# A linear-attention plus routed-MLP kernel: expert 0's first layer in batches of three, its weights fetched ahead of the last values, and a new written-out order

## The chip, the cores and the metric

The program runs on one core of one Trainium2 chip. That core has a matrix engine (TensorE, PE in the profile; PEld is its weight loads), a vector engine (VectorE, DVE), a scalar engine (ScalarE, ACT), a general engine that here issues nearly all transfers (GpSimd, POOL) and a small engine that issues the first few (SyncE, SP). The metric is the device time of one execution in microseconds; lower is better. The time before is 220.91 us, the median of 3 runs (220.52 to 221.06).

## What is computed

Two stages, one behind the other. The first is an attention without a score matrix: `q` is softened over the 64 features of a head, `k` over the 576 positions, and the product of `k` and `v` is one 64x64 matrix for each batch and head.

```
q_s = exp(q - max(q, -1)); q_s = q_s / (sum(q_s, -1) + 1e-09)
k_s = exp(k - max(k, 2));  k_s = k_s / (sum(k_s, 2) + 1e-09)
kv  = einsum('bhsd,bhse->bhde', k_s, v)
x   = einsum('bhsd,bhde->bhse', q_s, kv)          # 8 batches, 8 heads, 576 positions, 64
```

The second takes the 4608 rows of `x` (512 wide), gives each to one of 8 experts by a hash of its token's number, and runs that expert's two layers.

```
expert_idx = token_ids * 2654435761 % 8
for e in range(8):
    mask = expert_idx == e
    out[mask] = maximum(x[mask] @ w1[e], 0) @ w2[e]     # w1 512x1024, w2 1024x512
```

## The kernel before

Queries are never processed in their own order. The hash is ranked first (`_Index`), and the rows of `q` are gathered by expert: each expert has room for 640 rows, 72 from each of the 8 batches (576, `MAINC`) and 64 more (columns 576 to 640) for rows that exceed a batch's 72. These overflow rows come from four gathers of their own (expert "O"), are multiplied with their batch's key-value matrix in `overflow` and spread over the experts by one-hot matrices `Q` (`shared`, `spread`, `join`).

For a batch `b`, `K` and `V` load the keys and values, `EK` is the exponential on ACT, `KV` the 20 matmuls of keys with values (`keys`), and `SC` the division by the sums that leaves `kvr` (`scaled`, four DVE instructions). The sums come from a 129th column of ones beside each 128 value columns; `MK` (`mark`) writes that column on ACT. For an expert `e`, `G` are the gathers of 128 queries, `EQ` the exponentials, `SM` and `ML` the sums and the division on DVE, `TP` and `TC` the transposes on PE and their copies into `qT`, `PP` and `PC` the products with `kvr` and their copies into `XT`. `A` and `R` are the first layer and its relu (`first`, `relu`), `B` and `C` the second layer and its copy (`second`, `result`), `S` the scatter of 128 rows to the output.

Transfers of weights, `W<expert><layer>_<half>`, cast float32 to half precision in flight. The exponentials of the keys are stored in the tiles that later hold expert 1's weights. `ANY` is a branch into a slow path for the case that more than 64 rows overflow; each engine reads a flag, made in `CNT`, and jumps over that path. What is issued behind the branch waits until the engines that it depends on have passed the branch too.

All engines are scheduled by hand: the table `ORDER` lists some 700 steps, and each engine gets its instructions in the order in which the steps stand there. A name with `*n` puts n extra matmuls of 512 columns ahead of the step; their results are overwritten (`bank`). `SWAP` lists the copies that go to the other one of ACT and DVE. POOL therefore issues transfers strictly in the table's order, and each of its eight transfer semaphores is used again only when the transfer eight places earlier has landed.

PSUM has two buffers for each of three tags: "Q" and "T" (one bank each) and "S" (two banks: `keys`, and the first layer's larger pieces).

Expert 0's first layer is cut in columns 0 to 432 (four pieces `A0_0_0` to `A0_0_3`, eight matmuls each of 432 columns), 432 to 576 and 576 to 640. The first cut needs batches 0 to 5 and both halves of the weights.

Of the kernel before, what the change touches and what calls it, by code (L numbers as in the profile page):

```python
# [21 lines left out]
E_MOE = 8  # L22
# [285 lines left out]
class _Attention:  # L308

    def __init__(self, nc, tc, q, k, v, cpool, qpool, apool, ps):  # L310
# [4 lines left out]
        self.two = cpool.tile([128, VW - 128], F16, name="two")  # L315
        nc.vector.memset(self.two[:], 1.0)
# [118 lines left out]

    def product(self, qT, r, lo, hi, es, q0=0):
# [121 lines left out]
def _any_routing(nc, tc, q, k, v, token_ids, w1, w2, room, ident, w, ps, pool, out):  # L558
# [40 lines left out]
    with tc.For_i(0, NBP, 1) as n:  # L599
# [9 lines left out]
        nc.vector.memset(v16[:, :, 128:VW], 1.0)  # L609
# [17 lines left out]
        with tc.For_i(0, C9, 1) as c:  # L627
# [60 lines left out]
TC1_0 SD1 PC0_00 SD2 TCO_3 PC0_43 PC0_62 R0_0_3 TC2_0 C0_3 TC3_2 PC2_01 C0_0 PC2_02 C0_1 R1_320_1 C0_2 PC2_30  # L688
PC2_61 C2_0 PC4_31 C2_4 C4_2 PC6_31 C6_4 R7_0_0 C7_4a C7_4b
# [56 lines left out]
def kernel(  # L746
# [13 lines left out]
    with ExitStack() as fctx:  # L760
# [19 lines left out]
        with tc.manual_schedule(engines={eng.Pool, eng.PE, eng.DVE, eng.Activation}):  # L780
# [268 lines left out]
```

## Time and profile before

| what | value |
|---|---|
| median of 3 runs | 220.91 us |
| time of the profiled execution | 221.03 us |
| its span, first to last instruction | 219.3 us |
| PE busy | 187.9 us (86%) |
| DVE busy | 132.1 us (60%) |
| ACT busy | 114.8 us (52%) |
| POOL busy | 114.7 us (52%) |
| mean granted TensorE clock | 0.988 |
| bytes read from memory, written to it | 63.03 MB, 10.49 MB |

The span splits in two. Up to about 62 us the keys, values, queries and the first weights arrive, and all engines have gaps. From there to the last matmul PE has none. In the rows below "busy" of a group of matmuls includes the emptying of the pipeline, so that the time of one is read from the distance between starts, or from the chain of waits, which gives the undisturbed length of a piece. A transfer's row gives its size and the time from issue to landing; its issue stands in the rows of POOL.

### The profile page before, as it was taken

The page shows a single profiled execution, that of the slowest core. Times are in us where ns is not written, and L with a number is a line of the kernel's source. Part 1 is how long each engine was busy: PE and PEld are TensorE (multiplying, and loading weights), DVE is VectorE, ACT ScalarE, POOL GpSimd, SP SyncE. Part 2 cuts the span into 40 slices and gives each one's busy share as a digit, 9 for nine tenths or more (in the row PEclk, how much of TensorE's full clock was granted, in tenths as well). Part 3 has the DMA queues.
Part 4 walks back from the last instruction along what each step waited for, and adds up shares of the span by engine and source line. Part 5 has one row for each costly group of instructions (what it writes and reads, how often), then busy time and mean ns, then how long its engine had stood idle before and what let it go on. Part 6 is the DMA issues. An engine that isn't in the chain of part 4 may idle for free.

```text
span 219.3 us, 3984 instructions
## 1 busy us (share of the span) xinstructions
PE 187.9 (86%) x1534; PEld 122.0 (56%) x1534; DVE 132.1 (60%) x258; ACT 114.8 (52%) x184; POOL 114.7 (52%) x152
## 2 busy tenths in 40 slices
PE   3601098679899999999999999999999999999991
PEld 2501186347756865646676555667665566665540
DVE  6889689989969884659984505696324322021330
ACT  8125995799766674646465572436342432622201
POOL 7577876076367475558245407816055140833553
PEclk9999999699999999999999999999999999999998
DMA  6999999999999999999999924999769968595243
GB/s 207 308 324 314 335 396 384 227 326 306 231 336 258 269 247 319 293 216 200 249 209 212 206 80 83 211 219 269 176 145 226 237 144 187 144 167 212 96 153 119
DMA packets 12904, 50.64 MB, mean 231 GB/s; under 512 B 2522, under 2 KB 2522, under 8 KB 11344
## 3 DMA queue, kind: packets, MB, share of 16 engines
q0 software_dynamic: 12304, 46.63, 82.2%
q1 hardware_dynamic: 576, 3.71, 4.4%
q8 instruction: 13, 0.21, 0.4%
q14 instruction: 11, 0.09, 0.1%
HBM read 63.03 MB, written 10.49 MB: 335 GB/s over the span
## 4 chain that ended last, share of the span: by engine, by line
PE 64%; DVE 10%; issue 5%; POOL 4%; ACT 2%; POOLq 1%; DVEq 0%
PE ph L523 30%; PE po L545 25%; POOL out_dram L550 4%; PE t L432 3%; DVE kvr L388 2%; DVE qs L422 2%; PE px L455 2%; DVE rq L416 2%; PE t L443 2%; PE t L373 1%; ACT w1r L355 1%; PE t L472 1%; DVE XT L942 1%; DVE Q L280 1%; DVE XTov L478 1%
## 5 line engine op out<-in xcount | busy, mean ns | idle before, releaser
L545 PE MATMUL po<-w2r,hT 128*128 128x512 f16 (+2 forms) x328 | 74.6, 374 | 0.0
L523 PE MATMUL ph<-XT,w1r 128*128 128x320 f16 (+2 forms) x512 | 74.3, 298 | 0.0
L550 POOL DMA_INDIRECT out_dram<-ob,sidx x40 | 40.8, 1020 | 54.8 <-DVE ob L973 37.7
L536 ACT ACTIVATE hT<-ph 128x640 f16<-128x640 f32 (+3 forms) x60 | 42.4, 708 | 49.0 <-PE ph L523 48.9
L523 PEld LDWEIGHTS <-w1r 128*128 128x128 f16 x544 | 49.1, 98 | 20.7
L396 POOL DMA_INDIRECT raw<-in_q_dram,gidx x36 | 39.5, 1097 | 21.4 <-issue 6.8
L545 PEld LDWEIGHTS <-hT 128*128 128x128 f16 x328 | 31.1, 98 | 30.8
L973 DVE TENSOR_SCALAR ob<-po 128x512 f32<-128x512 f32 x31 | 21.1, 687 | 44.5 <-PE po L545 41.7
L416 DVE TENSOR_REDUCE rq<-qs 128x16 f32<-128x1024 f16 (+1 forms) x18 | 23.9, 1329 | 4.8 <-ACT qs L406 4.6
L406 ACT ACTIVATE qs<-raw 128x512 f16<-128x512 f32 x36 | 22.1, 630 | 5.6 <-DMA raw<-in_q_dram,gidx 4.8
L422 DVE TENSOR_TENSOR qs<-qs,rq 128x1024 f16<-128x1024 f16 (+1 forms) x18 | 23.9, 1326 | 0.1
L912 DVE COPY qT<-t 128x512 f16<-128x512 f16 (+1 forms) x18 | 9.3, 533 | 12.4 <-PE t L432 12.4
L432 PE MATMUL t<-ident,qs 128*128 128x128 f16 x160 | 14.2, 226 | 2.9 <-DVE qs L422 2.3
L432 PEld LDWEIGHTS <-qs 128*128 128x128 f16 x160 | 11.2, 101 | 5.2 <-ACT qs L406 2.5
L508 POOL DMA_DIRECT2D w2r<-in_moe_w_dram x14 | 8.2, 590 | 9.1 <-PE po L545 8.5
L948 ACT CAST XT<-px 128x864 f16<-128x864 f32 (+1 forms) x8 | 6.4, 819 | 11.6 <-PE px L455 11.5
L971 ACT ACTIVATE ob<-po 128x512 f32<-128x512 f32 (+2 forms) x10 | 5.5, 557 | 13.1 <-PE po L545 11.4
L355 ACT ACTIVATE w1r<-kraw 128x2048 f16<-128x2048 f32 x4 | 7.6, 1906 | 8.8 <-DMA kraw<-in_k_dram 8.8
L508 POOL DMA_DIRECT2D w1r<-in_moe_w_dram x15 | 8.8, 587 | 3.7 <-PE ph L523 2.0
L373 PE MATMUL t<-v,w1r 128*128 128x129 f16 x64 | 6.0, 244 | 5.4 <-ACTq L852 5.4
L942 DVE CAST XT<-t 128x288 f16<-128x288 f32 (+2 forms) x17 | 7.6, 459 | 4.4 <-PE t L443 4.3
L443 PE MATMUL t<-qT,kvr 128*128 128x72 f16 (+1 forms) x96 | 8.5, 206 | 1.0 <-DVE XT L942 0.7
(128 smaller groups left out, 186.2 us busy)
## 6 DMA issues: line engine op xcount, KB each, us to landing
w1r<-in_moe_w_dram POOLq DMA_DIRECT2D x14, 512.0 KB, 8.2
w2r<-in_moe_w_dram POOLq DMA_DIRECT2D x12, 512.0 KB, 9.2
kraw<-in_k_dram POOLq DMA_DIRECT2D x3, 1024.0 KB, 9.1
kraw<-in_k_dram SPq DMA_DIRECT2D x2, 1280.0 KB, 11.7
kraw<-in_k_dram POOLq DMA_DIRECT2D x2, 1280.0 KB, 10.9
w2r<-in_moe_w_dram POOLq DMA_DIRECT2D x2, 1024.0 KB, 9.4
v<-in_v_dram POOLq DMA_DIRECT2D x3, 645.0 KB, 8.2
v<-in_v_dram POOLq DMA_DIRECT2D x3, 516.0 KB, 10.3
```

Of the source, the lines that this page charges most:

```text
L396: nc.gpsimd.indirect_dma_start(out=raw[:, :], out_offset=None, in_=self.q[:, :], in_offset=bass.IndirectOffsetOnAxis(ap=idx[:, i:i + 1], a ...
L406: self.nc.scalar.activation(q16[:, i].rearrange("p h d -> p (h d)"), raws[i][:, :], ACT.Exp)
L416: nc.vector.reduce_sum(rv, qv, axis=AX.X)
L422: nc.vector.tensor_tensor(out=qf, in0=qf, in1=rv.rearrange("p i h -> p (i h)").unsqueeze(2) .to_broadcast([128, (hi - lo) * H_, DH_]), op= ...
L432: nc.tensor.transpose(pv[:, r, 128 * j:128 * j + 128], rq16[1][:, i + j, 2 * r:2 * r + 2, :] .rearrange("p h d -> p (h d)"), self.ident[:])
L443: nc.tensor.matmul(pv[:, :, i * CELL:(i + 1) * CELL], lhsT=self.kvrs[b][:, r, :], rhs=qT[:, r, q0 + es.start:q0 + es.stop, b * CELL:(b + 1 ...
L508: self.nc.gpsimd.dma_start(w[what - 1][:, f], src[e, :, f])
L523: nc.tensor.matmul(p, lhsT=w1r[:, dc, f[i] * 128:(f[i] + 1) * 128], rhs=X[:, dc, :], start=(dc == 0), stop=(dc == DC - 1))
L536: self.nc.scalar.activation(to, fro, ACT.Relu)
L545: nc.tensor.matmul(po[:, 0:d.stop - d.start], lhsT=hT[:, fc, blk * 128:(blk + 1) * 128], rhs=w2r[:, fc, d], start=(fc == 0), stop=(fc == F ...
L550: sc = self.nc.gpsimd.indirect_dma_start(out=self.out[:, :], out_offset=bass.IndirectOffsetOnAxis(ap=self.ix.sidx[:, e, blk:blk + 1], axis=0),
L973: nc.vector.tensor_scalar(out=obs[e, blk][:, d], in0=po[e, blk, x][:, 0:d.stop - d.start], scalar1=1.0 / SX, scalar2=None, op0=ALU.mult)
```

## The change

- **Order.** The table is another one, written anew from start to end. Expert 0's two `w1` transfers stand right behind `V4` and ahead of `V5`, `K6`, `K7`, `V6` and `V7`; before they stood behind all of them. The branch `ANY` stands ahead of `OHA` and `FND` (the search for overflow rows), before behind them. Extra matmuls: 52, before 24.
- **First layer of expert 0.** Columns 0 to 432 are cut in 0 to 216 and 216 to 432, which are batches 0 to 2 and 3 to 5. Each cut has two pieces of 16 matmuls of 216 columns.
- **Products of experts 0 and 1.** Two head pairs share one PSUM bank (`halves`), in batches 0 to 2, 3 to 5 and 6 to 7 for either expert: 12 copies in place of 20. The matmuls are the same 64.
- **Overflow queries.** They are no longer divided by their sums ahead of the product (`SMO`, `MLO` are gone). `overflow` has eight more matmuls of 2 columns for each pair of batches, which make the sums, and uses tag "S"; `normal` divides on DVE, in place of a copy.
- **Column of ones.** It is laid out with the values outside the program; the five `MK` copies on ACT are gone.
- `PAUSE` and `rest` are new, with an empty set: nothing is issued for them. The branch hint `HNT` is the table's first step.

```
-PARTS = ((0, slice(0, 1), ((0, 4), (4, 6), (6, 8))), (1, slice(1, 2), ((0, 4), (4, 8))),
-         *((e, slice(0, 2), ((0, 3), (3, 6), (6, 8))) for e in (2, 4, 6)))
-CUTS = [((0, 432), (432, MAINC), (MAINC, CAP))] + [((0, HN), (HN, CAP))] * (E_MOE - 1)
+THIRDS = ((0, 3), (3, 6), (6, 8))
+PARTS = tuple((e, slice(0, 2), THIRDS) for e in (2, 4, 6))
+CUTS = [((0, 216), (216, 432), (432, MAINC), (MAINC, CAP))] + [((0, HN), (HN, CAP))] * (E_MOE - 1)
...
+    def halves(self, qT, h, lo, hi, e):
+        px = self.bank("Q")
+        m = (hi - lo) * CELL
+        pv = px[:, 0:2 * m].rearrange("p (r i) -> p r i", r=2)
+        for r in range(2):
+            for b in range(lo, hi):
+                self.nc.tensor.matmul(pv[:, r, (b - lo) * CELL:(b - lo + 1) * CELL], lhsT=self.kvrs[b][:, 2 * h + r, :],
+                                      rhs=qT[:, 2 * h + r, e, b * CELL:(b + 1) * CELL], start=True, stop=True)
+        return pv
...
-    def overflow(self, n, qTo):
+    def overflow(self, n, qTo, ones):
         nc = self.nc
-        pt = self.bank("T")
+        pt = self.bank("S", (2, 512))
...
+        for r in range(NPAIR):
+            for j in range(2):
+                nc.tensor.matmul(pt[:, 1, 2 * r:2 * r + 2], lhsT=qTo[n][:, r, 64 * j:64 * j + 128],
+                                 rhs=ones[:, :, 0], start=(j == 0), stop=(j == 1))
         return pt
+
+    def normal(self, pt, xov, rq):
+        V = self.nc.vector
+        V.tensor_scalar(out=rq[:], in0=pt[:, 1, 0:H_], scalar1=1e-9, scalar2=None, op0=ALU.add)
+        V.reciprocal(rq[:], rq[:])
+        V.tensor_tensor(out=xov[:].rearrange("p (h d) -> p h d", h=H_), in0=pt[:, 0, :].rearrange("p (h d) -> p h d", h=H_),
+                        in1=rq[:].unsqueeze(2).to_broadcast([128, H_, DH_]), op=ALU.mult)
...
-    def mark(self, v16):
-        n = v16.shape[1]
-        self.nc.scalar.copy(v16[:, :, 128:VW], self.two[:].unsqueeze(1).to_broadcast([128, n, VW - 128]))
...
-                for x, lo, hi in (("a", 0, 2), ("b", 2, 4)) if n == 4 else (("a", 0, 3), ("b", 3, 5)):
+                for x, lo, hi in () if e == "O" else (("a", 0, 2), ("b", 2, 4)) if n == 4 else (("a", 0, 3), ("b", 3, 5)):
...
-            a = np.pad(a, ((0, 0),) * 4 + ((0, VW - 128),))
+            a = np.pad(a, ((0, 0),) * 4 + ((0, VW - 128),), constant_values=1)
...
-ML1b K7 MK4 PC0_02 V7 TP1_1 W01_1 SH3 SH1 TC1_1 PP0_00 PP0_01 W01_0 EK6 G2_0 SMOb KV5 PC0_01 TP1_2 SD1 SH2 PC0_00 MLOb
...
+SC0 K5 TCO_0 EQO_1 TPO_1 TCO_1 TC0_2 SM1a KV3 G1_3 ROP ML1a PP0_00 SM0b SC3 GO_2 EK4 TP1_0*7 TC1_0 V4 W01_1 PC0_00 XP0
```

POOL before, the transfers from the values of batch 4 on; a row is one transfer, `v_2` and `v_3` hold batches 4, 5 and 6, 7, the first `w1r` row is expert 0's, `raw` are gathers:

```order
L799 DMA v_2_824<-in_v_dram 128x2580
L799 DMA v_2_824<-in_v_dram 128x2064
L788 DMA kraw_913<-in_k_dram 128x2560
L799 DMA v_3_921<-in_v_dram 128x2580
L788 DMA kraw_924<-in_k_dram 128x2048
L799 DMA v_3_921<-in_v_dram 128x2064
L508 DMA w1r<-in_moe_w_dram 128x2048 x2
L396 DMA raw<-in_q_dram,gidx 128x512 x6
L508 DMA w1r<-in_moe_w_dram 128x2048
```

POOL after, from the same transfer on; here the first two `w1r` rows are expert 0's, the last two expert 1's, and `rawo` is the last gather of overflow rows:

```order
L820 DMA v_2_857<-in_v_dram 128x2580
L524 DMA w1r<-in_moe_w_dram 128x2048
L390 DMA raw<-in_q_dram,gidx 128x512
L524 DMA w1r<-in_moe_w_dram 128x2048
L820 DMA v_2_857<-in_v_dram 128x2064
L809 DMA kraw_971<-in_k_dram 128x2560
L809 DMA kraw_973<-in_k_dram 128x2048
L820 DMA v_3_1022<-in_v_dram 128x2580
L820 DMA v_3_1022<-in_v_dram 128x2064
L390 DMA rawo_285<-in_q_dram,oidx 128x512
L390 DMA raw<-in_q_dram,gidx 128x512
L524 DMA w1r<-in_moe_w_dram 128x2048
```

Expert 0's weights moved past five transfers of keys and values, which come that much later.

PE before, at the end of the first piece of expert 0's first layer; `kvr6` and `kvr7` are the matrices of the last two batches, so that all keys and values have been multiplied by then:

```order
L523 LDWEIGHTS w1r_295
L523 MATMUL ph_1228<-XT0_292,w1r_295 128x432
L472 LDWEIGHTS xov2_1175
L472 MATMUL t_1237<-Q_150,xov2_1175 128x512
L472 LDWEIGHTS xov3_1194
L472 MATMUL t_1237<-Q_150,xov3_1194 128x512
L443 LDWEIGHTS kvr6_107
L443 MATMUL t_1242<-qT_279,kvr6_107 128x72
```

PE after, at the end of the fourth and last piece of columns 0 to 432; the rows of line 367 are keys times values of batch 6 (`v16_3`):

```order
L539 LDWEIGHTS w1r_290
L539 MATMUL ph_1180<-XT0_286,w1r_290 128x216
L436 LDWEIGHTS kvr3_102
L436 MATMUL t_1197<-qT_273,kvr3_102 128x72
L436 LDWEIGHTS kvr4_103
L436 MATMUL t_1197<-qT_273,kvr4_103 128x72
L436 LDWEIGHTS kvr5_104
L436 MATMUL t_1197<-qT_273,kvr5_104 128x72
L436 LDWEIGHTS kvr3_102
L436 MATMUL t_1197<-qT_273,kvr3_102 128x72
...
L367 LDWEIGHTS w2r_293
L367 MATMUL t_1207<-v16_3_1022,w2r_293 128x129
```

All of the first layer's columns 0 to 432 moved ahead of the last two batches' keys and values.

## Rows read from the trace of the kernel before

**Rows 1.** View of stretches, three of them (columns in its first line).
```profile
core 0: us, PE busy (x) PEld busy (x) DVE busy (x) ACT busy (x) POOL busy (x), PEclk, DMA share, GB/s
5.50:62.50 57.00, 34.05 (x436) 26.37 (x437) 50.30 (x125) 38.95 (x61) 33.47 (x43) 0.97 1.03 319
62.50:214.30 151.80, 151.80 (x1092) 94.18 (x1089) 78.10 (x122) 70.67 (x115) 75.65 (x86) 1.00 0.84 203
41.00:42.00 1.00, 0.86 (x3) 0.31 (x3) 0.91 (x5) 1.00 (x4) 0.00 (x0) 0.50 1.08 217
```

**Rows 2.** Timeline of PE: start us, busy us, what, count, idle before.
```profile
26.92 0.59 PE L373 MATMUL t<-v,w1r 128*128 128x129 f16 x4 [5.39 <-ACTq L852]
...
39.88 1.01 PE L432 MATMUL t<-ident,qs 128*128 128x128 f16 x8 [2.35 <-DVE qs L422]
...
69.45 1.10 PE L523 MATMUL ph<-XTov,w1r 128*128 128x64 f16 x32
70.39 2.17 PE L523 MATMUL ph<-XT,w1r 128*128 128x144 f16 x32
72.61 0.57 PE L523 MATMUL ph<-XT,w1r 128*128 128x320 f16 x3
...
213.26 1.26 PE L545 MATMUL po<-w2r,hT 128*128 128x384 f16 x12
```

**Rows 3.** Timeline of POOL, issues of six transfers: start us, busy us, what.
```profile
37.84 0.53 POOL L799 DMA_DIRECT2D v<-in_v_dram  x1 [1.51 <-ACT qs L406]
...
44.71 0.53 POOL L788 DMA_DIRECT2D kraw<-in_k_dram  x1 [6.34 <-ACT w1r L355]
...
45.75 0.55 POOL L508 DMA_DIRECT2D w1r<-in_moe_w_dram  x1
46.27 0.56 POOL L508 DMA_DIRECT2D w1r<-in_moe_w_dram  x1
47.13 1.06 POOL L396 DMA_INDIRECT raw<-in_q_dram,gidx  x1 [0.30 <-issue]
...
65.43 0.62 POOL L508 DMA_DIRECT2D w2r<-in_moe_w_dram  x1
```

**Rows 4.** View of transfers, the same six: size, us to landing.
```profile
v<-in_v_dram POOLq DMA_DIRECT2D x1, 645.0 KB, 13.8
...
kraw<-in_k_dram POOLq DMA_DIRECT2D x1, 1024.0 KB, 9.4
...
w1r<-in_moe_w_dram POOLq DMA_DIRECT2D x1, 512.0 KB, 13.2
...
w1r<-in_moe_w_dram POOLq DMA_DIRECT2D x1, 512.0 KB, 15.2
...
raw<-in_q_dram,gidx POOLq DMA_INDIRECT x1, 15.0
...
w2r<-in_moe_w_dram POOLq DMA_DIRECT2D x1, 512.0 KB, 11.0
```

**Rows 5.** Chain of waits: start us, undisturbed length us, what.
```profile
26.92 2.34 PE t L373 x20
...
62.65 1.46 PE ph L523 x8
64.11 0.43 PE t L472 x2
...
72.55 0.22 PE t L432 x4
```

**Rows 6.** Timeline of DVE, the scaling of one batch, one division of overflow queries.
```profile
36.00 1.21 DVE L416 TENSOR_REDUCE rq<-qs 128x16 f32<-128x1024 f16 x1
...
57.88 0.69 DVE L478 CAST XTov<-t 128x512 f16<-128x512 f32 x1
...
58.70 0.15 DVE L382 TENSOR_SCALAR rec<-t 128x4 f32<-128x4 f32 x1
...
59.10 0.86 DVE L388 TENSOR_TENSOR kvr<-t,rec 64x256 f16<-64x256 f32 x2
```

More of the change, by code (lines that the diff above doesn't have):

```diff
@@ L824, in gather @@
                                            into=rawo if e == "O" else None))
+                rest(f"G{e}_{lo}")
             st = _Steps()
@@ L828 @@
             eng = mybir.EngineType
-            tc.mark_branch_hint_location("any", hint="LikelyTaken",
-                                         engines=[eng.PE, eng.DVE, eng.Activation, eng.Pool])
+            add("HNT", tc.mark_branch_hint_location, "any", "LikelyTaken", [eng.PE, eng.DVE, eng.Activation, eng.Pool])
             qT = qpool.tile([128, NPAIR, 4, MAINC], F16)
@@ L846, with rest @@
             flag = fpool.tile([128, 1], I32)
+            pause = fpool.tile([128, 512], F16)
+            def rest(name):
+                if name in PAUSE:
+                    nc.gpsimd.memset(pause[:], 0.0)
             muls, Qs, xovs = {}, [], {}
@@ L853, in anyway @@
                     _any_routing(nc, tc, q, k, v, moe_token_ids, moe_w1, moe_w2, (qT, XTs[0], hs[0], at.XTov),
-                                 at.ident, wts[0], ps, fpool, out)
+                                 at.ident, wts[max(wts, key=lambda e: e - e % 2 * E_MOE)], ps, fpool, out)
             add("ANY", anyway)
@@ L869 @@
                 add(f"EK{b}", expk, b)
-                if b % 2 == 0 or b - 1 not in PAIRS:
-                    add(f"MK{b}", mark, b)
                 add(f"KV{b}", lambda b: pkvs.update({b: at.keys(b, k16s, v16s)}), b)
@@ L918, in xovc @@
                     xovs[n] = tpool.tile([128, D_MOE], F16, name=f"xov{n}")
-                    (A if other(f"XC{n}", True) else V)(xovs[n][:], po["x", n][:])
-                add(f"XP{n}", lambda n: po.update({("x", n): at.overflow(n, qTo)}), n)
+                    at.normal(po["x", n], xovs[n], tpool.tile([128, H_], F32, name=f"rqo{n}"))
+                add(f"XP{n}", lambda n: po.update({("x", n): at.overflow(n, qTo, ix.ones)}), n)
                 add(f"XC{n}", xovc, n)
@@ L948, in prodsc, with half, halfc @@
                 (A if other(f"PC{e}_{lo}{h}", h == 0) else V)(xt(e // 2)[:, es, 2 * h:2 * h + 2, lo * CELL:hi * CELL], px[e, h, lo])
+            def half(e, h, lo, hi):
+                px[e, h, lo] = at.halves(qT, h, lo, hi, e)
+            def halfc(e, h, lo, hi):
+                (A if other(f"PC{e}_{lo}{h}", h == 0) else V)(xt(0)[:, e, 2 * h:2 * h + 2, lo * CELL:hi * CELL], px[e, h, lo])
+            for e in range(2):
+                for lo, hi in THIRDS:
+                    for h in range(2):
+                        add(f"PP{e}_{lo}{h}", half, e, h, lo, hi)
+                        add(f"PC{e}_{lo}{h}", halfc, e, h, lo, hi)
             for e, es, parts in PARTS:
@@ L974, in result, with scatter @@
                                             scalar1=1.0 / SX, scalar2=None, op0=ALU.mult)
+            def scatter(e, blk):
+                moe.scatter(e, blk, obs[e, blk])
+                rest(f"S{e}_{blk}")
             DS = {"": slice(0, D_MOE), "a": slice(0, 384), "b": slice(384, D_MOE)}
@@ L988 @@
                         add(f"C{e}_{blk}{x}", result, e, blk, x)
-                    add(f"S{e}_{blk}", lambda e, blk: moe.scatter(e, blk, obs[e, blk]), e, blk)
+                    add(f"S{e}_{blk}", scatter, e, blk)
             def room():
```

84 lines of the change are left out of this document (42 added, 42 removed).

## The prediction

> **What bounds the kernel now.** I read the stretches first. In [rows 1] the reader is to see two different machines. From 62.5 us to 214.3 PE is busy for 151.8 us of 151.8, at full clock: PE sets the pace, and no other engine is near it. From 5.5 to 62.5 PE is busy for 34 us of 57, while the transfer engines' share is 1.03, which is full. So the front part is set by the order in which bytes land, and by DVE (50.3 us of 57), and the back part by the amount of work that PE still has when it stops waiting. The end is therefore: the moment from which PE runs without a gap, plus PE's work from there, plus a tail. The tail is 219.3 less 214.52, where the last matmul ends [rows 2]: 4.8 us.
>
> Then the single transfers [rows 3, 4]: issue plus time to landing. Expert 0's two halves of `w1` land at 45.75 + 13.2 = 58.95 and 46.27 + 15.2 = 61.47, a gather at 47.13 + 15.0 = 62.13, the second half of expert 0's `w2` at 65.43 + 11.0 = 76.43. They land in the order of issue, one after the other. The first layer of expert 0 starts in the chain of waits at 62.65 [rows 5], 1.2 us behind its weights: before, PE's continuous part begins when those weights have landed, which were issued last. It is this that the new order moves.
>
> **Transfers.** Each transfer has a price, the distance between landings: half a `w1` or `w2` 61.47 - 58.95 = 2.52 us, a gather 62.13 - 61.47 = 0.66. Keys of batch 7 land at 54.11, values of batch 6 at 51.64, so those keys cost 2.47; values of batch 7 and half a `w1` fill 54.11 to 58.95, which leaves 2.3 for the values. By size, values of an even batch (645 against 516 KB) cost 2.9 and keys of an even batch 3.1. The new order has the same transfers ahead of expert 0's `w2` as the old one (keys, values, `w1` of experts 0 and 1, and the same number of gathers, though not the same ones), and the queue was never empty. So I take the landing of that `w2` as unchanged, 76.4, and count back through the new order. Behind the second half of expert 1's `w1` come six gathers and two halves of `w2`: that `w1` lands at 76.43 - 5.04 - 3.96 = 67.4. Behind the values of batch 7 come in all four weight halves, eight gathers and one overflow gather (0.4, an estimate between nothing and a full gather's 0.66): they land at 76.43 - 10.08 - 5.28 - 0.4 = 60.7, some 4 us later than before (54.11 + 2.3). Expert 0's `w1` stands a further 13 us ahead (2.3 + 2.9 + 2.5 + 3.1 + 2.3), at 47.6 instead of 61.5. The bound on each landing is 1.5 us later, if POOL's issue or its eight semaphores leave the queue empty once, and 0.5 earlier.
>
> **The front part.** PE's first keys-times-values waits 5.39 us for ACT to pass the branch, until 26.92 [rows 2]. With the branch earlier I put it at 21 us, behind one exponential of queries. That alone gives nothing at the end, since later steps wait for bytes; it makes room for the 28 more extra matmuls (at 0.216 each, half of 0.43 for two [rows 5], 6.0 us) and for the 5.9 us of first layer below. Under which the extra matmuls lie: waits for ACT, DVE and landings between 24 and 58 us. If that cover were gone, only the ones behind the last batches count: two, 0.43 us.
>
> First layer, columns 0 to 432: before 4 x 1.46 = 5.84 us [rows 5] in the continuous part. A matmul of 64 columns takes (70.39 - 69.45) / 32 = 29 ns, one of 144 columns (72.61 - 0.22 - 70.39) / 32 = 62.5 ns [rows 2, 5], one of 432 columns 182.5; on that line 216 columns cost 92.5, and 64 of them 5.9. So the split is free, and these 5.9 us leave the continuous part, since they need only batches 0 to 5 and weights that land at 47.6. The Trainium skill, page "TensorE: Matmul & The Clock Gate", section "Back-to-back issue gap", speaks against a split: for weight load and matmul in a stream it gives some 81 ns at 128 columns and 131 at 512, so that on its line 32 matmuls of 432 columns would cost 3.9 us and 64 of 216 columns 5.9, an estimate of 2.0 us more. The trace disagrees at both ends (62.5 ns at 144 columns, 182.5 at 432), and I stay with the rows; by the rule the sum would be 2.0 us higher.
>
> DVE: the division of overflow queries was two of reduce, add, reciprocal and multiply; the reduce is 1.21 us [rows 6], the multiply on the same 1024 columns taken as equal, with the small ones 5.7 in all. Now there are four divisions from PSUM, at the 0.69 of a 512-column copy from PSUM [rows 6] plus two small ones of about 0.15 each: 4.0. Of unknown sign within 2 us, and off the path as long as the values of batch 7 land last. The 32 new 2-column matmuls at 29 ns or less are 0.9 us, a fourth of it behind batch 7. The `MK` copies and the branch hint I cost at nothing: they stood beside ACT's waits for landings. Bounds for both: 1 us either way.
>
> **Where PE starts to run through.** Values of batch 7 at 60.7; keys times values 1.2 us (half of the 2.34 that 20 matmuls took at half clock [rows 5]): 61.9. The scaling on DVE from 58.70 to 59.96 is 1.3 [rows 6]: 63.2. Now the last products, about 0.5, an overflow product 0.6, the first layer's columns 432 to 576 (2.0) and one spread (0.43), with a copy to wait for in between: 67 us. There expert 1's first layer wants its second half of `w1`, 67.4 by the count above. The two arrive together; I take 67.6 with a little for the wait.
>
> Before, the first matmul of expert 1's first layer starts at 72.61, and 214.52 - 72.61 = 141.9 us of work follow [rows 2]. After, the same work follows, plus what the new order leaves behind that point: three spreads at 0.43, the overflow columns of expert 0 (70.39 - 69.45 = 0.94) and four transposes (0.22): 2.45. The last matmul ends at 67.6 + 141.9 + 2.45 = 212.0, against 214.52: 2.5 us less. Expert 0's second layer, 9.2 us behind the start of expert 1's first, would come at 76.8, with its `w2` landed at 76.4: just covered. Since three landings now stand within half a microsecond of use, and the part behind was free of any gap before, I give 0.2 back. The profiled execution took 221.03, 0.12 over the median of the runs; the sum is 221.03 - 2.3 = 218.7 in its terms, and 218.6 against the median. I forecast 218.7.
>
> **Rivals.**
> 1. The queue falls behind. Five gathers now stand ahead of the first values that POOL issues, and POOL takes 1.3 us for each (1.06 and 0.30 [rows 3]) where the queue needs 0.66; the same at the six gathers ahead of expert 0's `w2`. For it: two landings that feed PE directly have no reserve. Against it: eight transfers outstanding, and a share of 1.03 in the old order. At the 1.5 us bound everything from 67.6 on is that much later: 220.2, nearly all gain gone.
> 2. Slower: the clock. In the stretch from 41 to 42 us PE was granted half clock, behind an idle time of 2.35 us that ended at 39.88 [rows 1, 2]. Now PE may wait for expert 1's `w1` at 67 us, in front of 144 us of dense work. If that landing is over 2 us late (69.4 or later, the point from which it decides), PE both waits and comes back at half clock; at about 3.4 us of half clock (an estimate from the 41 to 42 row and the pieces around it, 39.9 to 43.3) it costs 1.7 more: 69.4 + 144.35 + 1.7 + 4.8 + 1.7 around the span is 222.0. Against it: a landing so late needs twice the shortfall of rival 1.
> 3. The first layer does not get ahead. Its pieces use the PSUM tag that keys-times-values and the overflow products use as well, two buffers, and their relus stand on ACT next to the exponentials of batches 6 and 7 (2.5 us each). If the two pieces of columns 216 to 432 slip behind batch 7, 3 us return: 221.6.
> 4. More than forecast: transfers land 0.5 earlier and overlap with other waits, or the old middle had losses that the search removed: 217.6. PE's 151.8 of 151.8 speaks against anything in the middle.
> The split's price by the skill's page would be a loss of up to 2.0 us where no wait covers it, 220.7; the rows leave it little.
>
> **How the numbers follow.** Forecast (217.9 to 219.7) 0.54; rival 1 (219.7 to 221.0) 0.17; rival 2 0.10; rival 3 0.06; rival 4 0.10; the split's price 0.03. About 0.3% (0.66 us) is what can be told from no change here: faster means below 220.25, slower above 221.57. Faster: 0.54 + 0.10 and half of rival 1, 0.73 with rounding; within: the other half of rival 1, the split's price and part of rival 3, 0.14; slower: rival 2 and the rest of rival 3, 0.13. The range for 8 in 10 leaves out half of rival 4 and most of the slower cases: 217.5 to 221.2.
>
> **What would show it.** Right: expert 0's `w1` landing near 47.6 and its 216-column matmuls done before batch 6; values of batch 7 landing near 60.7; expert 1's first layer starting at 67 to 68 with little idle time ahead, ended by a transfer; PE without a gap from there; 216 columns at 92 to 93 ns. Wrong: a start of expert 1's first layer beyond 69.5, half clock behind 60 us, or gaps on PE in the part behind 70 us, which the sum has at none.

## The result and the profile after

The changed kernel takes 223.46 us in the median of five runs, the kernel before 220.65 beside it; the ratio is 1.0126, with an interval of 1.0079 to 1.0174. It is slower, where 218.7 and a gain were forecast. A sixth run took 242.84 with a mean clock of 0.862; it is left out here, and nothing below rests on it. The five lie between 221.76 and 224.66, over a range of 2.9 us, where the runs of before lie within 0.6.

The profiled execution took 223.37 (span 221.4). Stretches, the ones of [rows 1]:

```profile
core 0: us, PE busy (x) PEld busy (x) DVE busy (x) ACT busy (x) POOL busy (x), PEclk, DMA share, GB/s
5.50:62.50 57.00, 42.23 (x507) 32.60 (x508) 47.08 (x118) 35.35 (x45) 30.84 (x42) 1.00 1.03 307
62.50:214.30 151.80, 148.57 (x1095) 92.75 (x1093) 90.40 (x137) 62.60 (x105) 77.65 (x85) 1.00 0.83 204
```

The front does what it was to do: PE is busy for 42.2 us of the 57 in place of 34.05. The back is no longer full: 148.57 of 151.8, where before it was 151.80. Timeline of PE, five of the rows with an idle time ahead of them (in brackets, with what ended it):

```profile
48.56 1.65 PE L539 MATMUL ph<-XT,w1r 128*128 128x216 f16 x16 [0.35 <-DMA w1r<-in_moe_w_dram]
...
62.30 0.39 PE L367 MATMUL t<-v,w2r 128*128 128x129 f16 x4 [1.20 <-DMA v<-in_v_dram]
...
97.79 0.41 PE L447 MATMUL t<-qT,kvr 128*128 128x144 f16 x4 [0.54 <-ACT XT L963]
99.50 0.72 PE L539 MATMUL ph<-XT,w1r 128*128 128x320 f16 x4 [1.30 <-DMA w1r<-in_moe_w_dram]
...
144.48 0.81 PE L561 MATMUL po<-w2r,hT 128*128 128x512 f16 x3 [1.10 <-DVE ob L1005]
```

Expert 0's `w1` is there at 48.5, and the four pieces run in the front. The first layer of expert 1 starts at 68.84; before, it started at 72.61. So 3.8 us were won by then. The same accounting as in the prediction, with what was measured:

| term | forecast | measured |
|---|---|---|
| first matmul of expert 1's first layer | 67.6 | 68.84 |
| PE's work from there | 144.35 | 144.36 (144.85 busy, less the 0.49 below) |
| idle time on PE behind it | 0 (0.2 given back) | 0.54 + 1.30 + 1.10 = 2.94 |
| emptying of PE's pipeline at these three waits, which counts as busy | 0 | 0.49 (0.16 at each) |
| tail, and time around the span | 4.8 + 1.7 | 4.77 + 1.97 |

The 144.85 is from the view of stretches:

```profile
68.84:216.63 147.79, 144.85 (x1021) 89.11 (x1018) 85.47 (x126) 60.36 (x101) 74.91 (x82) 1.00 0.81 201
```

From start to start of the matmuls, each of the three waits takes 0.16 us more than its idle time in the view.

The sum misses by 223.37 - 218.65 = 4.7 us: 1.2 in front of the work, 3.4 at the three waits (less the 0.2 given back), 0.2 in the last row, and nothing of it in the work itself.

Now the transfers. POOL's issues, and below them the view of transfers for the gathers issued at 69.84, 78.37, 80.36 and 81.67 and the half of `w2` at 83.46 (last column: us from issue to landing):

```profile
69.84 1.06 POOL L390 DMA_INDIRECT raw<-in_q_dram,gidx  x1 [0.30 <-issue]
...
75.16 1.00 POOL L390 DMA_INDIRECT raw<-in_q_dram,gidx  x1 [0.30 <-DMA w2r<-in_moe_w_dram]
76.46 1.00 POOL L390 DMA_INDIRECT raw<-in_q_dram,gidx  x1 [0.30 <-issue]
...
89.98 1.18 POOL L524 DMA_DIRECT2D w1r<-in_moe_w_dram  x2
```

```profile
raw<-in_q_dram,gidx POOLq DMA_INDIRECT x1, 8.3
...
raw<-in_q_dram,gidx POOLq DMA_INDIRECT x1, 6.0
...
raw<-in_q_dram,gidx POOLq DMA_INDIRECT x1, 4.6
...
raw<-in_q_dram,gidx POOLq DMA_INDIRECT x1, 5.4
...
w2r<-in_moe_w_dram POOLq DMA_DIRECT2D x1, 512.0 KB, 7.5
```

From 69.84 on six gathers stand in a row, and behind one half of `w2` three more. POOL issues one each 1.3 us in the row of six; the queue spends 0.66 on one [rows 3, 4]. The reserve, which is the time from issue to landing, falls from 8.3 to 4.6 us. Behind that, transfers land later than their prices allow: the gather issued at 81.67 lands at 87.1, 2.1 us behind the one ahead of it, and the half of `w2` at 91.0, another 3.9 us later, at a price of 2.5. The wait of 0.54 at 97.79 is of this kind too: the copy on ACT that PE waited for stands behind exponentials that waited for a gather. Timeline of ACT:

```profile
95.67 1.67 ACT L400 ACTIVATE qs<-raw 128x512 f16<-128x512 f32 x3 [1.38 <-DMA raw<-in_q_dram,gidx]
```

Stretches of the changed kernel (five rows), then of the kernel before (four):

```profile
77.00:81.00 4.00, 4.00 (x29) 2.36 (x28) 3.93 (x7) 2.23 (x5) 3.39 (x4) 1.00 1.03 346
82.00:84.00 2.00, 2.00 (x20) 1.46 (x19) 2.00 (x3) 1.44 (x3) 2.00 (x2) 1.00 0.89 291
83.00:91.00 8.00, 8.00 (x62) 4.79 (x60) 6.12 (x11) 4.60 (x9) 6.79 (x9) 1.00 0.93 230
85.00:87.00 2.00, 2.00 (x16) 1.18 (x15) 1.99 (x3) 1.97 (x4) 1.70 (x3) 1.00 1.04 197
20.00:23.50 3.50, 2.89 (x39) 2.77 (x40) 2.95 (x4) 3.38 (x5) 2.90 (x2) 1.00 0.90 203
```

```profile
54.00:58.00 4.00, 3.92 (x62) 3.43 (x60) 3.75 (x13) 3.87 (x6) 1.99 (x2) 1.00 1.07 214
82.00:84.00 2.00, 2.00 (x16) 1.06 (x14) 1.71 (x4) 0.00 (x0) 0.88 (x2) 1.00 1.07 350
83.00:91.00 8.00, 8.00 (x60) 4.69 (x58) 3.64 (x7) 4.87 (x10) 4.20 (x5) 1.00 1.05 312
20.50:23.50 3.00, 0.65 (x18) 0.56 (x18) 2.02 (x10) 2.98 (x4) 2.39 (x3) 1.00 1.02 303
```

The share (the column before the last) shows where the queue is thin: 0.89 at 82 to 84, where POOL is busy for all of the 2.00 us, against 1.07 in the old order, where POOL is busy for 0.88. The last column does not show it. The 197 GB/s at 85 to 87 is what weights bring, at a full share of 1.04: at 54 to 58 of the kernel before values and weights bring 214 at 1.07. The 346 at 77 to 81 is a stretch of gathers. Over 83 to 91 the share is 0.93 in place of 1.05, which is about 1 us of the queue's time (an estimate: 8 us times 0.12), less than the waits of 0.54 and 1.30 with their emptying; what the rest of them hangs on is not shown. The Trainium skill, page "Perfetto Trace Analysis", section "DMA Optimizations", describes the case in which the making of transfers is the limit: the issuing engine looks busy with issues, rather than the transfers themselves taking the time. The two rows at 82 to 84 agree with it.

Something like it happened once earlier: five gathers stand ahead of the values of batch 2, the row at 20 to 23.5 has a share of 0.90 where the old order had 1.02, and the landings lost 2.6 us against their prices between 20 and 27 us. (In the next profile of the same kernel the share there is 0.99, so that the landings carry this and not the share.)

The wait at 144 is another one. Timeline of POOL, then of DVE:

```profile
130.35 0.59 POOL L524 DMA_DIRECT2D w1r<-in_moe_w_dram  x1 [6.88 <-PE px L459]
132.34 0.56 POOL L524 DMA_DIRECT2D w2r<-in_moe_w_dram  x1 [1.39 <-PE po L561]
132.89 0.54 POOL L524 DMA_DIRECT2D w1r<-in_moe_w_dram  x1
133.73 1.04 POOL L566 DMA_INDIRECT out_dram<-ob,sidx  x1 [0.30 <-DVE XT L969]
```

```profile
143.73 0.69 DVE L1005 TENSOR_SCALAR ob<-po 128x512 f32<-128x512 f32 x1 [4.40 <-DMA out_dram<-ob,sidx]
```

A scatter stands behind three halves of weights and lands at 143.6; the output tile that it holds is the next one that DVE needs, DVE holds the PSUM bank that PE needs.

### The profile page after: what moved, and what is told of

Same layout as the page of the kernel before. It is cut to its first block, busy times and chain, and to the rows that moved or that the text cites. A ratio compares the mean times of both kernels' runs of the same rounds, so it can differ in the third digit from the quotient of the medians.

```text
span 221.4 us, 4151 instructions
## 1 busy us (share of the span) xinstructions
PE 194.9 (88%) x1626; PEld 128.2 (58%) x1626; DVE 141.1 (64%) x266; ACT 103.9 (47%) x160; POOL 115.6 (52%) x152
## 4 chain that ended last, share of the span: by engine, by line
PE 29%; DMA 27%; issue 17%; POOL 9%; ACT 4%; DVE 2%; POOLq 1%; ACTq 0%; DVEq 0%
PE ph L539 14%; PE po L561 11%; DMA raw<-in_q_dram,gidx 8%; DMA kraw<-in_k_dram 7%; POOL out_dram L566 6%; DMA out_dram<-ob,sidx 4%; DMA w1r<-in_moe_w_dram 4%; DMA rawo<-in_q_dram,oidx 4%; POOL raw L390 2%; ACT qs L400 2%; PE t L426 2%; PE px L459 1%; PE t L367 1%; POOL w1r L524 1%; POOLq L1080 1%
## 5 line engine op out<-in xcount | busy, mean ns | idle before, releaser
L539 PEld LDWEIGHTS <-w1r 128*128 128x128 f16 x576 | 51.8, 98 | 21.5 <-DMA w1r<-in_moe_w_dram 2.0
L552 ACT ACTIVATE hT<-ph 128x640 f16<-128x640 f32 (+3 forms) x32 | 22.2, 709 | 48.9 <-PE ph L539 48.9
L554 DVE TENSOR_SCALAR hT<-ph 128x640 f16<-128x640 f32 (+2 forms) x31 | 25.7, 833 | 30.2 <-PE ph L539 30.0
L1003 ACT ACTIVATE ob<-po 128x512 f32<-128x512 f32 (+2 forms) x24 | 13.6, 581 | 28.4 <-PE po L561 28.4
L410 DVE TENSOR_REDUCE rq<-qs 128x16 f32<-128x1024 f16 (+1 forms) x16 | 21.5, 1344 | 5.8 <-ACT qs L400 5.8
L416 DVE TENSOR_TENSOR qs<-qs,rq 128x1024 f16<-128x1024 f16 (+1 forms) x16 | 21.5, 1350 | 0.1
L1005 DVE TENSOR_SCALAR ob<-po 128x512 f32<-128x512 f32 x17 | 11.5, 683 | 9.8 <-DMA out_dram<-ob,sidx 4.4
L344 PE MATMUL t<-rowi,ident 128*128 128x512 f16 x52 | 15.1, 423 | 0.0
L933 ACT COPY qT<-t 128x512 f16<-128x512 f16 (+1 forms) x15 | 10.7, 728 | 2.8 <-PE t L426 2.7
L969 DVE CAST XT<-px 128x864 f16<-128x864 f32 (+1 forms) x7 | 6.7, 970 | 8.2 <-PE px L459 8.2
```

Source lines behind the costliest of these rows:

```text
L344: self.nc.tensor.matmul(t[:, 0, :] if len(shape) > 1 else t[:], lhsT=self.ident[:], rhs=self.rowi[:, 0:512], start=True, stop=True)
L410: nc.vector.reduce_sum(rv, qv, axis=AX.X)
L416: nc.vector.tensor_tensor(out=qf, in0=qf, in1=rv.rearrange("p i h -> p (i h)").unsqueeze(2) .to_broadcast([128, (hi - lo) * H_, DH_]), op= ...
L539: nc.tensor.matmul(p, lhsT=w1r[:, dc, f[i] * 128:(f[i] + 1) * 128], rhs=X[:, dc, :], start=(dc == 0), stop=(dc == DC - 1))
L552: self.nc.scalar.activation(to, fro, ACT.Relu)
L554: self.nc.vector.tensor_single_scalar(to, fro, 0.0, ALU.max)
```

## The experiments

Two theories were put against each other. Q: the transfers' order costs the time, in two thin stretches of the queue and at one scatter. S: the new instructions cost it. The steps of the table are moved by their names: `V2` values of batch 2, `G5_1` a gather of expert 5, `W12_1` the second half of expert 1's `w2`, `S2_1` a scatter, `A0_576_0` the 64-column piece. They ran in five groups, each group on one chip with its own runs of before (medians 220.65 to 220.85); the first two groups have the same chip number. Only runs of one group are compared in microseconds, since the changed kernel itself differed between groups, as will be seen.

**First group.**

> The changed kernel once more, as the one that the next three are compared with. Theory Q (the order of transfers lets the queue run dry between 80 and 92 us, because POOL issues a gather each 1.3 us and the queue needs 0.66 for one; a scatter behind weights holds an output tile at 143): 223.9, with PE idle for about 1.8 us between 97 and 99.5 and 1.1 at 143. Rival S (the new instructions themselves, split matmuls, extra matmuls and 2-column matmuls, cost the time): 223.9, and PE busy longer than before by some 5 us behind 69 us.

223.66 (221.79 to 225.1), ratio 1.0119 (1.0088 to 1.0151). The profiled execution (225.1) had its wait at another place, 2.04 us at 90.90. Timeline of PE and of ACT:

```profile
90.90 0.38 PE L426 MATMUL t<-ident,qs 128*128 128x128 f16 x4 [2.04 <-ACT qT L933]
```

```profile
89.75 0.63 ACT L400 ACTIVATE qs<-raw 128x512 f16<-128x512 f32 x1 [3.64 <-DMA raw<-in_q_dram,gidx]
```

ACT waits for a late gather (`G5_1`), and the copy behind it on ACT is what PE waits for. Q said 97 to 99.5: a late transfer is what ended the chain, as Q had it, but at another place. That the place changes from run to run because the late queue meets whichever consumer comes first is an argument; no run tests it.

```
-... G5_2 R0_576_0 W12_0 B0_1 ML2a G4_4 ... G5_1 ... G4_3 ... W12_1 ... S0_1 ... W21_1 ...
+... W12_1 G5_2 R0_576_0 W12_0 B0_1 ML2a G4_4 ... W21_1 G5_1 ... G4_3 ... S0_1 ...
```

> Two transfers of the changed kernel issued earlier: the second half of expert 1's w2 ahead of four gathers, the first half of expert 2's w1 ahead of five transfers. Q: the queue keeps bytes outstanding from 77 to 92 us, the last half of expert 2's w1 lands at about 96 in place of 99.45, the idle of 1.8 us at 97 to 99.5 goes and the one at 143 stays: 222.0. S: 223.9, since no instruction is taken away.

227.45 (226.86 to 229.26), 3.8 worse than the control. The weights landed early as expected (the last half at 95.6), but `G5_1` stood behind 5 us more of bytes. Timeline of ACT, timeline of PE, stretches:

```profile
90.14 0.63 ACT L400 ACTIVATE qs<-raw 128x512 f16<-128x512 f32 x1 [5.70 <-DMA raw<-in_q_dram,gidx]
```

```profile
91.29 0.59 PE L426 MATMUL t<-ident,qs 128*128 128x128 f16 x4 [4.10 <-ACT qT L933]
```

```profile
91.29:93.00 1.71, 1.71 (x11) 1.34 (x11) 1.57 (x5) 1.71 (x4) 0.00 (x0) 0.50 1.04 254
93.00:95.00 2.00, 2.00 (x13) 1.44 (x11) 0.00 (x0) 0.23 (x1) 0.33 (x1) 0.50 0.65 129
```

4.10 us of waiting, and then half clock (0.50, 1.2 GHz). Q's forecast failed, because it looked at the weights' deadline and not at the gather's. It is still no support for S: nothing but two transfers moved.

```
-... C2_1 W51_1 PP4_30 ... W42_1 W51_0 PC4_31 SM6b C2_3 S2_1 S0_4
+... C2_1 W51_1 S2_1 S0_4 PP4_30 ... W42_1 W51_0 PC4_31 SM6b C2_3
```

> Two scatters of the changed kernel issued ahead of two halves of weights, in place of behind them (at 131 us). Q: the output tile comes free some 7 us earlier, the idle of 1.1 us at 143 goes and the one at 97 to 99.5 stays: 222.8. S: 223.9.

222.64 (221.22 to 223.26), ratio 1.0100 (1.0086 to 1.0115): 1.0 below the control, as expected, though the intervals overlap. The profile decides it; PE at the place of the old wait:

```profile
142.55 1.89 PE L561 MATMUL po<-w2r,hT 128*128 128x512 f16 x8
144.28 1.25 PE L539 MATMUL ph<-XT,w1r 128*128 128x320 f16 x8
```

No wait is left there. The same holds later: in the eight profiles with these two scatters moved PE never waits for the scatter, and in the nine with the new back and the scatters in place it waits 0.31 to 1.44 us. But the idle time at 97 to 99.5, which was to stay, was 0.25 us here. No transfer ahead of 130 us had moved, so that the idle time between 85 and 100 varies by itself, from 0.25 to 2.04 us.

```
 (steps of the changed kernel up to G3_3)
-A1_0_2 SI1 W02_1 A1_0_0 R1_0_2 EQ2_2 SI3 ...
+SI1 W02_1 EQ2_2 SI3 W02_0 ... SE3 A0_576_0 OV1 G5_2 G4_4
+A1_0_0 A1_320_3 SM2a TP3_0 ... (from here the order of the kernel before)
```

> The changed kernel up to the start of expert 1's first layer, and from there the steps in the order of the kernel before (with its choice of engines); the steps that the old order has done by then (five of spreads, three gathers' worth of exponentials, w2 of expert 0, one transpose and the last columns of expert 0) stand ahead of it. Q: the front gives its gain, expert 1's first layer starts at 69 to 70 with these steps done, and the old back has no idle over 0.5: 220.5 to 221.0. S: 223.9, the instructions of the front are all there.

225.94 (225.09 to 227.78). Behind expert 1's start there is no idle time at all. But the steps that I had to put ahead of it stand in a row there and wait for DVE (1.02, 0.37, 0.54, 0.56 and 0.35 us), expert 1 starts at 75.87, and with so late a start the old back is no test. Neither theory is told apart; the run shows only that these steps in a row cost 2.8 us of waiting.

**Second group**, without a control, which was a mistake: the next group shows that the changed kernel itself can take longer.

```
-... CNT G0_1 OVA G1_1 EQ0_1 G0_0 G0_2 V2 ANY
+... CNT G0_1 V2 OVA G1_1 EQ0_1 G0_0 G0_2 ANY
```

> The changed kernel with the values of batches 2 (one transfer, issued at 18.5 us behind five gathers) issued behind the second gather. Theory Q: of the 2.6 us that the queue lost between 20 and 27 us (landings later than the sum of their prices) about 2 come back, expert 1's second half of w1 lands near 66.7 in place of 68.7, expert 1's first layer starts near 67: 221.7. Rival S (the new instructions cost the time, not the transfers): 223.7.

```
-... SI2 G6_4 A1_0_1 ... G5_0 A0_576_0 G5_3 G6_1 TC3_0 ... B1_2 G6_0 PC2_62
+... SI2 A1_0_1 ... G5_0 A0_576_0 G5_3 TC3_0 ... B1_2 G6_0 G6_4 G6_1 PC2_62
```

> The changed kernel with two gathers of expert 6, issued at 70 and 75 us and used behind 112 us, put behind the weights of experts 2 and 3. Q: 2.6 us of POOL's issuing and 1.3 us of the queue go from the stretch ahead of 85 us, so that the queue does not run dry there: the third gather of expert 5 lands near 83 in place of 85 to 90, ACT's exponential and expert 2's weights are in time, and PE's idle time between 85 and 100 (1.8 to 2.0 us) goes: 221.8; the wait for the scatter at 143 stays. S: 223.7.

The third run makes these two moves and that of the scatters.

> Values of batch 2 early, expert 6's two gathers late, and two scatters ahead of weights (as in the run of the scatters), together. Q: the sum of the three, 223.7 less 2.0, less 1.9, less 1.0: 218.8, with less than 0.5 us of idle time on PE behind 70 us. S: 223.7.

```
-PAUSE = set("""
-""".split())
+PAUSE = set("""
+G6_4 G2_3 G5_0 G5_3 G6_1 G5_2
+""".split())
```

> The changed kernel with a small memset on POOL behind each of six gathers issued between 70 and 78 us: the suspected cost made larger (0.3 to 0.5 us each by other small POOL work, an estimate). No transfer is moved. Q: the queue runs dry earlier and longer, the gathers that ACT waits for land 1.8 to 3 us later, and PE's idle time between 85 and 100 grows by as much: 225.5 to 226.7. S, and whoever thinks that the bytes alone set the landings: 223.7.

224.89 (223.67 to 225.14 in three runs, 228.81 to 230.56 in three others), 225.99 (225.32 to 226.83), 222.96 (221.90 to 224.99) and 228.27 (227.83 to 228.54). By the microseconds all four are over what Q forecast. What the idle time on PE between 85 and 140 us says is mixed. With the memsets it is 3.2 us, at the same copy of ACT as in the first group, plus 0.14. Timeline of PE, then stretches:

```profile
92.80 0.38 PE L426 MATMUL t<-ident,qs 128*128 128x128 f16 x4 [3.21 <-ACT qT L934]
```

```profile
82.00:84.00 2.00, 2.00 (x17) 1.08 (x15) 1.93 (x5) 1.59 (x3) 1.70 (x4) 1.00 0.42 123
```

So a slower POOL, with no transfer moved, empties the queue (a share of 0.42, where it was 0.89) and makes PE wait there. There is no idle time with the gathers of expert 6 late and none with the three moves, as Q said; but there is none with `V2` early either, where all nine gathers stayed and Q left the wait as it was. That moving two gathers takes the wait away is therefore not shown by this group.

**Third group**, with a control.

> The changed kernel again, as control for the next three, since the chip of the last four runs showed waits of 0.4 us inside runs of matmuls on PE that no transfer or engine ends. Theory Q (transfers) and rival S (new instructions): 223.7 on a chip without such waits, 225 to 226 on one with them.

> The three moves again (values of batch 2 early, two gathers of expert 6 late, two scatters ahead of weights), now beside a control. Q: no idle time on PE between 85 and 146 us; against the control 1.8 to 2.0 for the gathers and weights, 0.7 to 1.1 for the scatter, 1 to 2 for the earlier landings in the front: 3.5 to 5 us less, 218.7 to 220.2 where the control takes 223.7. S: as the control.

> Two of the three moves: the gathers of expert 6 late and the scatters early, the values of batch 2 as in the changed kernel. Q: 2.5 to 3 us less than the control, 220.7 to 221.2; the first layer of expert 1 starts where the control's does. S: as the control.

```
-... V4 W01_1 ... W01_0 V5 KV4 K6 K7 ... V6 ... V7 TP1_3 ...
+... V4 ... V5 KV4 K6 K7 ... V6 ... V7 W01_1 W01_0 TP1_3 ...
 (and A0_0_1 A0_0_0 A0_216_0 A0_216_1 with their relus behind PC0_60)
```

> The headline of the change undone inside the changed kernel: expert 0's two w1 transfers behind the values of batch 7, and its four pieces of 216 columns behind the first products of batches 6 and 7. Q: values of batch 7 land 5 us earlier, expert 1's first layer starts 2 to 2.5 us later than in the control, but the transfers behind 70 us stay where they are, so the idle time at 85 to 100 (1.8 to 2.0) shrinks by as much: 0 to 0.8 over the control. That the front's gain comes through whole, whatever stands behind it: 2 to 2.5 over the control. S: as the control, with the idle time unchanged.

| run | median us (range) | ratio to before (interval) |
|---|---|---|
| control | 232.39 (230.27 to 233.42) | 1.0514 (1.0479 to 1.0550) |
| three moves | 225.80 (225.65 to 226.69) | 1.0232 (1.0213 to 1.0251) |
| two moves | 224.76 (223.26 and 226.26; four others 226.80 to 230.17) | 1.0177 (1.0124 to 1.0229) |
| w1 behind the values | 232.71 (231.72 to 234.29; another 235.34) | 1.0541 (1.0512 to 1.0571) |

The control itself takes 8.7 us more than in the first group, where before stays at 220.85. Its PE stands still inside its 64-column matmuls, and then runs at half clock. Timeline, then stretches:

```profile
79.52 0.25 PE L539 MATMUL ph<-XTov,w1r 128*128 128x64 f16 x3 [0.54 <-issue]
...
82.46 0.43 PE L539 MATMUL ph<-XTov,w1r 128*128 128x64 f16 x5 [1.19 <-issue]
83.92 0.53 PE L539 MATMUL ph<-XTov,w1r 128*128 128x64 f16 x7 [1.03 <-issue]
```

```profile
84.00:86.00 2.00, 2.00 (x14) 1.27 (x14) 1.98 (x2) 1.18 (x2) 0.55 (x1) 0.50 0.96 272
```

"issue" means that nothing in the profile ended the pause. Against this control the three moves are worth 6.6 us, more than Q's 3.5 to 5, and S, which gave nothing, falls as the whole cause: no instruction was taken away. But the 6.6 are not the price of Q's waits: the control's profile has none over 0.34 us between 85 and 146, and lost time to the pauses and the half clock behind them. Two moves spread too much to be told from three. With `w1` put back, the total is 0.3 over the control, within Q's 0 to 0.8. But that run is a poorer test than it looks. In its profiled execution (235.34) the last gather of overflow rows now stood behind both halves of `w1`, PE waited 4.11 us for its exponential, and expert 1 started at 80.51, 8.6 us later than the control's 71.87 and not 2 to 2.5. And its PE shows none of the control's pauses, which alone are 3.9 us in the 64-column piece. So it does not price the move of `w1`.

**Fourth group.** What was still open: whether the kernel before has the pauses too, whether they belong to the 64-column matmuls or to the moment, and whether the three moves come under before.

> The kernel before, for its profile beside the others of this call. If the pauses come with small matmuls wherever the chip shows them (theory P), its 64-column run and the 72-column products show some too, but their time lies in front of its 151.8 us of dense work: 220.8 with pauses of under 1 us in total behind 62 us. If they come with the changed kernel's placement alone: none.

> The changed kernel as control. 223.7 without the pauses, 230 to 232 with them; in both cases idle time between 85 and 100 or half clock behind a longer idle, and 0.3 to 1.1 at the scatter.

> The three moves of transfers. Without the pauses: expert 1's first layer at 68, 219 to 220; with them 225.8 as before. Q: below the control by 3.5 to 6.6 either way, no idle on PE between 85 and 140.

```
-... TP3_1 ... G5_0 A0_576_0 G5_3 ... R1_320_1 TC3_1 G5_2 R0_576_0 W12_0 B0_1 ... B0_2 ... C0_2 EQ5_0
+... TP3_1 ... G5_0 G5_3 ... R1_320_1 TC3_1 G5_2 W12_0 B0_1 ... B0_2 ... C0_2 A0_576_0 R0_576_0 EQ5_0
```

> The three moves, and the 32 matmuls of 64 columns of expert 0's first layer 5 us later, behind two blocks of its second layer. Theory P (the pauses belong to runs of short matmuls): they move along, same time as the three moves alone. Rival T (they belong to the moment, to what the queue and the other engines do at 77 to 80 us): the pauses there go, 1.5 us less than the three moves alone where those show pauses; equal where they don't.

220.74; 226.26 (226.08 to 227.73, and a fourth of 231.52), ratio 1.0275 (1.0226 to 1.0323); 222.36 (221.92 to 224.52), ratio 1.0084 (1.0049 to 1.0119); 222.96 (222.44 to 223.12), ratio 1.0086 (1.0059 to 1.0113). Stretches behind expert 1's start, of before and of the three moves:

```profile
72.10:214.00 141.90, 141.90 (x980) 87.43 (x977) 69.81 (x109) 64.12 (x103) 68.31 (x76) 1.00 0.83 200
```

```profile
69.90:214.30 144.40, 144.40 (x1021) 89.10 (x1018) 85.28 (x126) 59.71 (x100) 72.76 (x81) 1.00 0.83 200
```

The three moves give the back without a gap that the forecast took for granted, 144.40 of 144.40, and take 3.9 us from the control. Here too the control had next to no idle time where Q saw the gathers' fault:

```profile
85.00:140.00 55.00, 54.92 (x402) 34.40 (x401) 41.78 (x64) 29.55 (x53) 30.92 (x36) 1.00 0.96 216
```

It starts expert 1 1.6 us later (71.50), and loses 0.86 at the scatter and 0.9 in pauses at 78 to 80 us. Before shows no pause behind its expert 1 start. What keeps the three moves above it stands in two places. PE behind the last keys times values, and POOL's last issue; after the latter the same row of the changed kernel's first profile:

```profile
64.33 0.27 PE L436 MATMUL t<-qT,kvr 128*128 128x72 f16 x3 [0.42 <-issue]
65.07 0.29 PE L436 MATMUL t<-qT,kvr 128*128 128x72 f16 x4 [0.47 <-issue]
...
68.68 0.39 PE L488 MATMUL t<-Q,xov 128*128 128x512 f16 x1 [0.68 <-DVE xov L482]
```

```profile
216.22 0.98 POOL L566 DMA_INDIRECT out_dram<-ob,sidx  x1 [1.64 <-ACT ob L1003]
```

```profile
217.22 0.98 POOL L566 DMA_INDIRECT out_dram<-ob,sidx  x1 [0.39 <-ACT ob L1003]
```

From the last keys times values (61.49) to expert 1's start it is 8.4 us here and 6.5 (62.30 to 68.84) in the first profile, and the tail is 5.9 in place of 4.8. Neither place belongs to the three moves. The control has the same 8.4 and 5.9; in every profile of the changed kernel in the last four groups the tail is 5.9 to 6.5, in the first comparison and the first group 4.7 to 4.8. So they come and go with the groups, as the pauses do. The fourth run does not tell P from T, since in this group the 64-column piece of the three moves ran without pauses too.

**Fifth group.**

```
-... TPO_3*2 ... SI0 A0_432_0 G3_2 R0_432_0 SE0 G2_2 EQ2_4 G3_3 A1_0_2 SI1
+... TPO_3 ... A0_432_0 G3_2 R0_432_0 G2_2 EQ2_4 G3_3 A1_0_2 SI0 SE0 SI1
 (and C7_1 C7_2 C7_3 on DVE)
```

> The three moves, and besides: the spread that waits for the last overflow division (0.7 us in the run before) one piece of expert 1's first layer later, the two extra matmuls ahead of the last transposes gone (0.43), and three of the last output copies on DVE as in the kernel before, so that ACT has only the last two. If the late tail (5.9 us behind the last matmul against 4.8) comes from copies in a row on ACT, it goes back to 4.8: 222.4 less 0.7, 0.4 and 1.1: 220.2. If it comes from elsewhere (rival): 221.3.

> The three moves alone, as control for the other run: 222.4 with the pauses, 219 to 219.5 without.

223.40 (223.09 to 224.23) against 222.82 (222.21 to 224.72): no gain. The tail stays at 6.0 with the copies on DVE, so the rival holds: it comes from elsewhere. The wait of 0.7 and the two matmuls were taken away, and other waits of 0.34 to 0.95 came in the same stretch, so that expert 1 starts at 69.63 and not earlier. No version here beats the kernel before. The three moves were not run in a group without the pauses; there their time would be near 219.0, under before (an estimate: 222.12 of the profiled run, less 1.9 and 1.2 for the two places). That is not shown.

## Why the prediction was wrong

- **Expert 0's `w1` and its first pieces: right.** It lands at 48.5 (47.6 forecast), the pieces run before the keys and values of batch 6, and 216 columns cost 93 ns (92.5). The split is free: 64 matmuls of 216 columns take 5.93 us where 32 of 432 took 5.84. The price that the Trainium skill gives for it (page "TensorE: Matmul & The Clock Gate", section "Back-to-back issue gap") does not show up.
- **The branch: right.** The first keys times values start at 20.6 (21).
- **PE's work behind expert 1's start: right**, 144.36 against 144.35.
- **Keys times values: right in size**, 1.14 us at 62.30 against 1.2. The prediction halved a row "at half clock"; the granted clock of that row (26.92 to 29.26) reads 1.00, and why its matmuls took 0.11 us each and 0.057 later stays open.
- **Landings counted back from expert 0's `w2` as unchanged: wrong.** This step held that the queue was never empty, which it took from the old order. In the new one the second half of that `w2` lands at 77.5 in place of 76.4, expert 1's `w1` at 68.7 in place of 67.4, and the values of batch 7 at 62.2 in place of 60.7, at the edge of the bound of 1.5 us. POOL's issues and the times to landing of that `w1` and `w2`:

```profile
54.97 0.57 POOL L524 DMA_DIRECT2D w1r<-in_moe_w_dram  x1 [1.20 <-PE t L436]
...
68.98 0.56 POOL L524 DMA_DIRECT2D w2r<-in_moe_w_dram  x1 [1.05 <-DMA w1r<-in_moe_w_dram]
```

```profile
w1r<-in_moe_w_dram POOLq DMA_DIRECT2D x1, 512.0 KB, 13.7
...
w2r<-in_moe_w_dram POOLq DMA_DIRECT2D x1, 512.0 KB, 8.5
```

It is the values that set expert 1's start: from their keys times values PE has 6.5 us to it with one wait of 0.24, and the `w1` is there. That is rival 1, at the place that it named: with `V2` moved ahead of three of the five gathers the last keys times values start between 61.2 and 61.6 in all seven profiles that have it, against 62.0 to 63.8 in the ten others that keep the rest of the front in its order. How the five gathers delay it is less sure, since the share in that stretch is full in some of the ten.
- **"PE's 151.8 of 151.8 speaks against anything in the middle": the step that failed most.** It is a row of the old order. The table was written anew to the end, and I checked the new one's transfers only up to expert 0's `w2`. Behind that, PE waits three times, 2.94 us, which cost 3.4 with the emptying of its pipeline. One wait, 1.10, is for a scatter behind three halves of weights. This is shown: it is gone in all eight profiles with the scatters moved. The other two, 1.84, are for a gather and a half of `w1` that landed late behind nine gathers within 14 us, which POOL issues at half the queue's pace. I had counted the 1.3 us of POOL against the 0.66 of the queue, and used it only for the landings ahead of `w2`. The rows show the late landings, and a slower POOL makes the wait longer (3.2 us). That fewer gathers take it away is not shown: it is gone in all eight profiles with two gathers late, but it is also gone in three without that (`V2` early, and the controls of the third and fourth group) and 0.25 in the run of the scatters.
- **The rivals.** Rival 2, half clock behind expert 1's start, is not what happened in the first profile (1.00 throughout), but it did elsewhere: PE came back at half clock behind the wait of 4.10 us, and behind the pauses of the third group's control. Behind waits of 2.04 and 3.21 us it came back at 1.00, so that a wait of over 2 us did not decide it. Rivals 3 and 4 fell.
- **The range** ended at 221.2. It took the bound of 1.5 us on landings from one place and had no term for the part behind.

Open: the pauses. In the last four groups they are in every profile of a changed kernel but the one with `w1` put back; they are in none of the first comparison and the first group, and not in the one of the kernel before. The chip alone does not explain them: the second group has them and carries the chip number of the first, which has none. Nearly all landings are missing from the records of the last four groups, also in the two profiles without pauses, so that a pause that "nothing ended" is weak evidence. Whether the pauses belong to the recording, to the moment, or to the density of short instructions was not settled. They do not decide the verdict: in the first comparison and the first group, whose profiles have none, the changed kernel was slower by 1.2 to 1.3%. They do decide what is left over: whether the new front with the transfers put right would beat the kernel before is open.

## What to carry to other kernels

Where an order is written anew, go through its transfers to the end, with two clocks: when the issuing engine can issue each one, and what the queue needs for it. Rows of the old order are no evidence for a stretch that was reordered. A run of gathers on one issuing engine can eat the reserve of a queue; look at the time from issue to landing, and at the busy share in stretches of 2 us, against the same rows of the kernel before. GB/s is no measure of it, since it changes with the kind of transfer. Before a run is called proof that a move took a wait away, look whether the control beside it had the wait. And a transfer has a deadline not only at the engine that reads it: an engine that works in order passes its wait on to whoever is next.

## What the runs showed of the hardware

- A gather costs POOL 1.3 us (1.00 and 0.30 between) and the queue 0.66; a half of `w2` issued when a gather's time from issue to landing was down to 4.6 us landed 1.4 us later than its price.
- At a full share the queue moved 214 GB/s of values and weights (54 to 58 us of the kernel before, 1.07) and 346 in a stretch of gathers (77 to 81 of the changed one, 1.03).
- Behind 4.10 us of waiting PE ran at 0.50 from 91.29 to past 95 us; behind 2.04 and 3.21 us, in two other runs, at 1.00.
- Pauses of 0.4 to 1.2 us on PE inside runs of short matmuls, ended by nothing in the profile, in four of the five groups: up to 3.9 us in one 64-column piece of 0.9 us, with ACT idle for 3 us in it.
